# A gated scan feeding a mixture of experts: query transfers issued from GpSimd, a written order of VectorE and ScalarE in the first block, and attention later in ten periods

## The chip, the cores and the metric

The kernel runs on one core of a Trainium2 chip. The metric is the device time of one execution in microseconds (us); smaller is better. The engines of the core are TensorE (PE in the profile, its weight loads PEld), VectorE (DVE), ScalarE (ACT), GpSimd (POOL) and SyncE (SP). SyncE, ScalarE and GpSimd can issue transfers (DMAs); an engine works through its own instructions strictly in the order in which they were queued, and waits where an instruction's inputs are not there.

## What is computed

The reference, cut to what matters. The first part is a linear attention with a complex gate at each step of time, the second a layer of eight experts whose weights are made by eight rounds of normalising rows and columns:

```python
def _attn_ref(q, k, v, a_re, a_im):          # 4 x 8 heads, 768 steps, head dim 48
    mag = np.sqrt(a_re * a_re + a_im * a_im)
    scale = np.minimum(mag, 0.999) / (mag + 1e-06)
    a_re_n, a_im_n = (a_re * scale, a_im * scale)
    for t in range(S):
        ar, ai = (a_re_n[:, :, t, :, None], a_im_n[:, :, t, :, None])
        new_re = ar * S_re - ai * S_im
        new_im = ar * S_im + ai * S_re
        kv = np.einsum('bhd,bhe->bhde', k[:, :, t], v[:, :, t])
        S_re, S_im = (new_re + kv, new_im)
        y[:, :, t] = np.einsum('bhd,bhde->bhe', q[:, :, t], S_re)

def _moe_ref(x, w_gate, w1, w2):             # x: 3072 x 384, 8 experts, 1024 wide
    P = np.exp(x @ w_gate - (x @ w_gate).max())
    for _ in range(8):
        P /= P.sum(1, keepdims=True) + 1e-09
        P /= P.sum(0, keepdims=True) + 1e-09
        P *= N / E
    for e in range(E):
        out += P[:, e:e + 1] * (np.maximum(x @ w1[e], 0.0) @ w2[e])
```

All is in 32-bit floats; a matrix product is made of three products of a high and a low part of its operands.

## The kernel before, in words

**Blocks and periods.** The 3072 tokens are worked through in 12 blocks of 256 (`SUB`), each of two chunks, or halves, of 128 (`CH`). Phase 1 (`phase1`, lines 212 to 305) computes the attention of all blocks and the first two experts; phase 2 (from line 688) does the normalising and the other six experts. Phase 1 goes in periods: period i holds the 16 expert steps of block i-1 (two experts of eight slices) and, between them, the attention of block i.

**What a block's attention needs.** `elem(i)` (line 328) loads gates, queries, keys and values and calls `chain` (line 389), which runs on VectorE and ScalarE: the gates are normalised (lines 402 to 418), multiplied up along time by a scan of complex multiplications (`scan`, `cmul`, lines 307 to 387, temporaries `cm_a` and `cm_b`), and made into scaled keys `kh` (line 436) and queries `z` (line 438). Blocks 0 and 1 do the steps around the scan separately for the two halves, later blocks for both at once.

**The attention itself** is `mix(i)` (line 441), a generator: `next(mix)` emits one piece of it, five for a chunk, ten for a block. For each chunk it moves six pieces of `kh` to `ks` and six of `z` to `qs` by DMA (line 455), all issued by SyncE, keys ahead of queries. `keys(g)` transposes keys for a half g of the heads (line 474) and ScalarE copies them out (`kt`, line 476); `scores(g)` multiplies keys and queries (line 488) and VectorE copies the scores under a mask (line 491, the masked copy); `state(g)` makes the new state's part `U` (line 483); `outs(g)` gives the outputs from masked scores and from the old state (line 505). VectorE then makes the next state (lines 531 to 542), ScalarE writes the outputs' high part `xh` (line 544) and VectorE the low part `xl` (line 545). The pieces are: keys(0) and scores(0); state(0) and keys(1); outs(0) and scores(1); state(1); outs(1) with the state and xh, xl.

**An expert step** is a generator too (`experts`, line 169): nine products of the first layer (`ph`, lines 201 to 203), for each of three column groups one with weights' high part and xh, one with xl, one with the weights' low part and xh; then two activations on ScalarE (`hh`, `hf`) and a subtraction on VectorE (`hl`, line 209). The second layer's six products (`po`, lines 180 to 182) of a step come `LAG` = 3 steps later; three steps are pending at any time. `send((None, 1, None))` emits the second products of one pending step alone.

**The order.** TensorE's instructions keep the program's order (`manual_schedule`, line 114). Those of the other engines are put in order by a planner that simulates the program with its own costs; `issue_after(x)` tells it to put an instruction behind x. `LEAD` (line 27) says at which expert step of period i the pieces of `mix(i)` begin, one behind each step; what is left of the ten when the 16 steps are over comes behind them (line 297), and there, for the blocks named in `LEAD`, second products of a pending step follow each piece while there are any. Before, `LEAD` names blocks 1 to 3 (steps 11, 8 and 5); all others begin at step 4.

**The first block** has no expert steps beside it. Its loop (lines 262 to 280) emits the ten pieces of `mix(0)`, and between them five of the weight splits that `thirds` (line 144) has prepared; three come ahead. A split takes a third of a slice's weights: the load (line 151), a cast to its high part on GpSimd (line 152), two products on TensorE (lines 156 and 157) and a copy of the low part on ScalarE (line 159). `elem(1)` is planned behind block 0's, and `behind` (line 277) puts its twelve complex multiplications behind marks in block 0's masked copies and xl.

Of the kernel before, what the change touches and what calls it, by code (L numbers as in the profile page):

```python
# [60 lines left out]
class Net:  # L61
# [81 lines left out]

    def thirds(self, e, fs, wx, late):
# [3 lines left out]
        def one(t, f, j):  # L148
# [3 lines left out]
            nc.gpsimd.tensor_copy(t[:, 0, cs], raw)  # L152
# [16 lines left out]
    def experts(self):  # L169
# [18 lines left out]
        while True:  # L188
# [10 lines left out]
            for ct in range(NCT):  # L199
                cs = slice(ct * 128, ct * 128 + 128)  # L200
                nc.tensor.matmul(ph, w[:, 0, cs], xh[:, ct, :], start=(ct == 0), stop=False)  # L201
                nc.tensor.matmul(ph, w[:, 0, cs], xl[:, ct, :], start=False, stop=False)  # L202
                nc.tensor.matmul(ph, w[:, 1, cs], xh[:, ct, :], start=False, stop=(ct == NCT - 1))  # L203
# [103 lines left out]
    def cmul(self, L, R, n, alloc):  # L307
# [8 lines left out]
        with ExitStack() as st:  # L316
            if self.behind:
                st.enter_context(self.tc.issue_after(self.behind.pop(0).ins))
            for o, k in ((a, 0), (b, 1)):
                if len(sh) == 4:  # L320
                    V.tensor_tensor(o, L, R[:, k:k + 1].broadcast_to(sh), ALU.mult)
                else:
                    for j in range(2):
                        V.tensor_tensor(o[:, j], L[:, j], R[:, k], ALU.mult)
        V.tensor_tensor(R[:, 0], a[:, 0], b[:, 1], ALU.subtract)
        V.tensor_tensor(R[:, 1], a[:, 1], b[:, 0], ALU.add)
# [62 lines left out]
    def chain(self, i, parts, zt, qk, alloc):  # L389
# [6 lines left out]
        for n in parts or [None]:  # L396
            f0, f1 = (base + i, base + 2 + i) if n else (i, ns + i)
            sq_, x_, y_, zz_, z_ = (t if n is None else half(t, n) for t in (sq, x, y0, zz, z))
            with ExitStack() as st:
# [2 lines left out]
                nc.scalar.activation(sq_, z_, AF.Square, accum_out=fl[:, f0:f0 + 1])
            with ExitStack() as st:
                if i == 2:
                    st.enter_context(tc.issue_after(self.zl[1, 1].ins))
                V.scalar_tensor_tensor(x_, sq_[:, 0], 1e-20, sq_[:, 1], ALU.max, ALU.add)
            with ExitStack() as st:
                if i == 1 and n == 0:
                    st.enter_context(tc.issue_after(self.ev[2].ins))
                nc.scalar.activation(y_, x_, AF.Abs_reciprocal_sqrt)  # L410
            nc.scalar.activation(zz_, y_, AF.Square, accum_out=fl[:, f1:f1 + 1])
            V.tensor_tensor(x_, x_, zz_, ALU.mult)
            V.scalar_tensor_tensor(y_, x_, -3.0, y_, ALU.add, ALU.mult)
# [622 lines left out]
```

## Time and profile before

| | |
|---|---|
| three runs | 1822.3, 1822.61 and 1824.88 us, median 1822.61 |
| the profiled execution | 1822.66 us, its span 1820.8 us |
| mean granted TensorE clock | 0.994 of full speed |
| idle of TensorE by what ended it | queries `qs` 5.4 us in 2 waits, `xl` 5.3 in 4, keys `ks` 4.0 in 1, `xh` 1.9 in 2, masked scores 1.6 in 3 |
| query and key transfers | 144 of each, 64.5 and 64 KB, 2.2 us from issue to landing |
| transfers issued by GpSimd | none |

A line of the timeline gives start and length in us, engine, line of the kernel, operation, output and input, and how many like it were merged (x6); a bracket gives the idle time before it and what ended it. SPq is SyncE's queue of issued transfers: its length is the time that issuing took. A line of the waits gives who waited for whom, in total, how often and the longest. "Granted clock" is the share of TensorE's full speed in a stretch.

### The profile page before, as it was taken

How to read it: one execution, taken by the hardware profiler on the slowest of the kernel's cores; microseconds unless marked ns; L12 is line 12 of the kernel's file. 1: busy time of each engine (PE TensorE's matmuls, PEld its weight loads, DVE VectorE, ACT ScalarE, POOL GpSimd, SP SyncE). 2: the span in 40 equal slices, each digit the busy share in tenths (PEclk: the TensorE clock that was granted, in tenths of full speed). 3: DMA queues.
4: the chain of work that ended last, by engine and by line, in shares of the span. 5: the costliest groups of instructions: out<-in, count | busy, mean ns of one | idle time of the engine just before them, and what ended most of it. 6: DMA issues, size and time to landing. Idle time of an engine off the chain costs nothing.

```text
span 1820.8 us, 30541 instructions
## 1 busy us (share of the span) xinstructions
PE 1765.5 (97%) x12024; PEld 1725.9 (95%) x12024; DVE 1359.6 (75%) x3023; ACT 729.1 (40%) x1592; POOL 16.3 (1%) x29
## 2 busy tenths in 40 slices
PE   5899999999999999999999999999999999999998
PEld 3889899999999999999999999998999999999998
DVE  8899899888873687868575867677776767675754
ACT  7444444554543433334342434243433334242421
POOL 3000000000000000000000000000000000000000
PEclk9999999999999999999999999999999999999999
DMA  6434343333332421401020101231220101020100
GB/s 208 113 108 118 109 115 118 109 107 115 113 102 99 131 87 48 126 18 53 1 70 1 54 17 53 74 105 65 87 70 18 53 18 53 1 70 1 53 27 28
DMA packets 120631, 132.83 MB, mean 73 GB/s; under 512 B 9632, under 2 KB 100512, under 8 KB 120480
## 3 DMA queue, kind: packets, MB, share of 16 engines
q1 hardware_dynamic: 119680, 130.41, 23.4%
q8 instruction: 96, 1.57, 0.4%
q14 instruction: 55, 0.45, 0.1%
q10 hardware_dynamic: 800, 0.39, 0.1%
HBM read 88.22 MB, written 23.59 MB: 61 GB/s over the span
## 4 chain that ended last, share of the span: by engine, by line
PE 83%; DVE 9%; DMA 4%; SPq 1%; issue 1%; ACT 1%; DVEq 0%; ACTq 0%
PE po L761 10%; PE po L759 10%; PE po L760 10%; PE P L798 9%; PE P L800 9%; PE P L799 9%; PE po L180 3%; PE ph L202 3%; PE ph L203 3%; PE ph L201 3%; PE po L182 3%; PE po L181 3%; PE sp L488 2%; PE y L505 2%; DMA raw<-in_w_dram 2%; PE U L483 1%
## 5 line engine op out<-in xcount | busy, mean ns | idle before, releaser
L761 PE MATMUL po<-wc,hl 128*128 128x384 f32 x1152 | 385.3, 334 | 3.0 <-DVE hl L820 3.0
L759 PE MATMUL po<-wc,hh 128*128 128x384 f32 x1152 | 385.0, 334 | 0.1
L760 PE MATMUL po<-wc,hh 128*128 128x384 f32 x1152 | 384.9, 334 | 0.0
L819 ACT ACTIVATE hh<-c 128x384 fp32r<-128x384 f32 x384 | 200.9, 524 | 322.2 <-DVE c L808 320.8
L820 DVE SCALAR_TENSOR_TENSOR hl<-c,hh 128x384 fp32r<-128x384 f32 x384 | 211.9, 552 | 65.9 <-ACT hh L819 58.0
L761 PEld LDWEIGHTS po<-wc,hl 128*128 128x128 f32 x1152 | 216.3, 188 | 4.3 <-DVE hl L820 4.3
L759 PEld LDWEIGHTS po<-wc,hh 128*128 128x128 f32 x1152 | 216.3, 188 | 0.4 <-ACT hh L819 0.4
L760 PEld LDWEIGHTS po<-wc,hh 128*128 128x128 f32 x1152 | 216.3, 188 | 0.0
L813 ACT ACTIVATE s<-P 128x384 f32<-128x384 f32 x192 | 94.2, 490 | 274.2 <-PE P L800 274.2
L207 ACT ACTIVATE hh<-ph 128x256 fp32r<-128x256 f32 x192 | 73.4, 382 | 248.2 <-PE ph L203 247.5
L202 PE MATMUL ph<-xl,w 128*128 128x256 f32 x576 | 163.9, 285 | 5.3 <-DVE xl L545 5.3
L201 PE MATMUL ph<-xh,w 128*128 128x256 f32 x576 | 163.0, 283 | 1.9 <-ACT xh L544 1.9
L203 PE MATMUL ph<-xh,w 128*128 128x256 f32 x576 | 163.2, 283 | 0.0
L798 PE MATMUL P<-B,wa 128*128 128x384 f32 x480 | 160.5, 334 | 1.3 <-DVE u L808 0.7
L800 PE MATMUL P<-B,wa 128*128 128x384 f32 x480 | 160.4, 334 | 0.0
L799 PE MATMUL P<-B,wa 128*128 128x384 f32 x480 | 160.3, 334 | 0.0
L180 PE MATMUL po<-w,hh 128*128 128x384 f32 x384 | 140.7, 366 | 0.9 <-ACT yst L185 0.9
L182 PE MATMUL po<-w,hl 128*128 128x384 f32 x384 | 130.0, 338 | 0.0
L808 DVE TENSOR_TENSOR c<-P,u 128x384 f32<-128x384 f32 x192 | 106.2, 553 | 31.3 <-PE P L800 30.2
L181 PE MATMUL po<-w,hh 128*128 128x384 f32 x384 | 129.4, 337 | 0.0
L808 DVE TENSOR_TENSOR u<-u,s 128x384 f32<-128x384 f32 x96 | 53.3, 556 | 101.0 <-ACT s L813 100.9
L202 PEld LDWEIGHTS ph<-xl,w 128*128 128x128 f32 x576 | 110.0, 191 | 6.2 <-DVE xl L545 6.2
(173 smaller groups left out, 3625.2 us busy)
## 6 DMA issues: line engine op xcount, KB each, us to landing
raw<-in_w_dram SPq DMA_DIRECT2D x48, 768.0 KB, 4.3
qs<-z SPq DMA_DIRECT2D x144, 64.5 KB, 2.2
qk<-in_aqk_dram SPq DMA_DIRECT2D x12, 768.0 KB, 5.0
ks<-kh SPq DMA_DIRECT2D x144, 64.0 KB, 2.2
ye_d<-yst SPq DMA_DIRECT2D x48, 192.0 KB, 1.9
y<-ye_d SPq DMA_DIRECT2D x48, 192.0 KB, 2.4
z<-in_aqk_dram SPq DMA_DIRECT2D x11, 768.0 KB, 7.3
B<-x_d SPq DMA_DIRECT2D x40, 192.0 KB, 3.6
```

The lines of the kernel that those rows point to most:

```text
L180: nc.tensor.matmul(po[k], hh[:, s], w2h, start=f == 0, stop=False)
L201: nc.tensor.matmul(ph, w[:, 0, cs], xh[:, ct, :], start=(ct == 0), stop=False)
L202: nc.tensor.matmul(ph, w[:, 0, cs], xl[:, ct, :], start=False, stop=False)
L203: nc.tensor.matmul(ph, w[:, 1, cs], xh[:, ct, :], start=False, stop=(ct == NCT - 1))
L759: nc.tensor.matmul(po[k], hh[:, s], w2[:, 0, i], start=first, stop=False)
L760: nc.tensor.matmul(po[k], hh[:, s], w2[:, 1, i], start=False, stop=False)
L761: nc.tensor.matmul(po[k], hl[:, s], w2[:, 0, i], start=False, stop=last)
L798: nc.tensor.matmul(ps, t[:, 0, k], x[:, 0], start=first, stop=False)
L799: nc.tensor.matmul(ps, t[:, 0, k], x[:, 1], start=False, stop=False)
L800: nc.tensor.matmul(ps, t[:, 1, k], x[:, 0], start=False, stop=last)
L819: A.activation(hh, c, AF.Relu)
L820: V.scalar_tensor_tensor(hl, c, 0.0, hh.bitcast(F32), ALU.max, ALU.subtract)
```

## The change

Four things are changed.

1. The query transfers are issued from GpSimd's queue, the key transfers stay on SyncE's. Queries of the second chunk are planned behind those of the first. `ql`, behind which later loads are planned, now means the last key transfer.
2. In block 0 (`i == 0`) the pieces are put together anew, four to a chunk: keys(0) and keys(1); scores(0) and state(0); scores(1) and state(1); outs(0) and outs(1) with the rest. The splits come at other places: three ahead, three between the pieces, two behind. The first expert step of each block (`e == 0 and f == 0`) does its six products with xh ahead of the three with xl.
3. Of the twelve casts of the splits the fourth to eighth (`mid`) go from GpSimd to ScalarE. The order of VectorE from block 0's queries to block 1's third complex multiplication, and of ScalarE up to block 0's first `kt`, is written out by hand, with `add_manual_dep` between neighbours; `behind` and the marks go. In this list p0 and p1 are the steps that make keys and queries of block 0's halves, n0 and n1 the normalising of block 1's, m0 and m1 the masked copies, state and xl of block 0's chunks, cm the complex multiplications of block 1.
4. `LEAD` names blocks 1 to 10, with later steps.

```diff
-LEAD = {1: 11, 2: 8, 3: 5}
+LEAD = {1: 13, 2: 13, 3: 12, 4: 11, 5: 9, 6: 8, 7: 7, 8: 6, 9: 6, 10: 5}
...
             nc.sync.dma_start(raw, self.w[e, f, :, cs])
-            nc.gpsimd.tensor_copy(t[:, 0, cs], raw)
+            n = self.nthird
+            self.nthird += 1
+            mid = HEAD <= n < 2 * (LAG + 1)
+            if not mid:
+                nc.gpsimd.tensor_copy(t[:, 0, cs], raw)
 
             def split():
+                if mid:
+                    with self.tc.issue_after(self.kt.ins):
+                        nc.scalar.activation(t[:, 0, cs], raw, AF.Copy)
...
-            for ct in range(NCT):
-                cs = slice(ct * 128, ct * 128 + 128)
-                nc.tensor.matmul(ph, w[:, 0, cs], xh[:, ct, :], start=(ct == 0), stop=False)
-                nc.tensor.matmul(ph, w[:, 0, cs], xl[:, ct, :], start=False, stop=False)
-                nc.tensor.matmul(ph, w[:, 1, cs], xh[:, ct, :], start=False, stop=(ct == NCT - 1))
+            terms = [(ct, k, x) for ct in range(NCT) for k, x in ((0, xh), (0, xl), (1, xh))]
+            if e == 0 and f == 0:
+                terms.sort(key=lambda t: t[2] is xl)
...
-                    if n in (0, 2, 3, 5, 7):
+                    if n in (2, 3, 6):
                         splits.pop(0)()
-                    if n == NF - LAG + 1:
+                    if n == 5:
                         for load in loads:
...
-                with tc.issue_after(self.gl.ins), tc.issue_after(g1.ins):
-                    m = self.marks
-                    self.behind = [m[j] for j in (0, 0, 0, 2, 2, 2, 3, 3, 3, 4, 5, 5)]
+                splits.pop(0)()
+                splits.pop(0)()
+                edge = mybir.DependencyInfo(mybir.DependencyClass.NoSync, mybir.DependencyReason.DATA)
+                with tc.issue_after(g1.ins):
                     self.elem(1)
-                edge = mybir.DependencyInfo(mybir.DependencyClass.NoSync, mybir.DependencyReason.DATA)
+                p0, p1, n0, n1 = (self.dve[k] for k in ((0, 0), (0, 1), (1, "n0"), (1, "n1")))
+                m0, m1, cm = self.dve["m", 0], self.dve["m", 1], self.dve["c"]
+                order = p0 + [n0[0], n1[0]] + p1 + [n0[1], n1[1], n0[2], n1[2], m0[0], n0[3], n1[3], m0[1], n0[4]] + n0[5:]
+                order += m0[2:] + [n1[4], m1[0]] + n1[5:] + cm[:4] + [m1[1]] + cm[4:8] + [m1[-1]] + m1[2:-1] + cm[8:9]
+                for a, b in zip(order, order[1:]):
+                    tc.add_manual_dep(b.ins, a.ins.name, edge, reason="order of VectorE")
+                a0, a1, ev = self.act[1, 0], self.act[1, 1], self.ev[2 * NF + 2:]
+                order = [g1] + ev[:2] + [a0[0], a1[0]] + ev[2:4] + [a0[1], a1[1], a0[2], a1[2]] + ev[4:8] + self.act["kt", 0, 0]
+                for a, b in zip(order, order[1:]):
+                    tc.add_manual_dep(b.ins, a.ins.name, edge, reason="order of ScalarE")
...
+        last = {}
         for c in range(NCH):
...
+            pre = dict(last)
...
-                        dma = nc.sync.dma_start(dst[q:q + D - 2:NCT, :, :w], src[:, a, ct * NCH + c, :w])
-            self.ql[i] = dma
+                        eng = nc.gpsimd if dst is qs else nc.sync
+                        with ExitStack() as st:
+                            if dst is qs and c:
+                                st.enter_context(self.tc.issue_after(pre["q"].ins))
+                            dma = eng.dma_start(dst[q:q + D - 2:NCT, :, :w], src[:, a, ct * NCH + c, :w])
+                        last["q" if dst is qs else "k"] = dma
+                        if dst is ks:
+                            self.ql[i] = dma
...
             keys(0)
+            if i == 0:
+                keys(1)
+                yield
             scores(0)
-            yield
-            state(0)
-            keys(1)
-            yield
-            outs(0)
-            scores(1)
-            yield
+            if i == 0:
+                state(0)
+                yield
+                scores(1)
+            else:
+                yield
+                state(0)
+                keys(1)
+                yield
+                outs(0)
+                scores(1)
+                yield
             state(1)
...
+            if i == 0:
+                outs(0)
             outs(1)
```

The rest of the diff collects the instructions into the lists `dve`, `act` and `ev` from which the two orders are written, and drops the `issue_after` in `cmul` and in the normalising of block 1.

More of the change, by code (lines that the diff above doesn't have):

```diff
@@ L198, in experts @@
             ph = self.psA.tile([128, SUB], F32, tag="ph", name=f"ph{e}_{i}_{f}")
[L199 to L203 removed]
+            terms = [(ct, k, x) for ct in range(NCT) for k, x in ((0, xh), (0, xl), (1, xh))]
+            if e == 0 and f == 0:
+                terms.sort(key=lambda t: t[2] is xl)
+            for q, (ct, k, x) in enumerate(terms):
+                nc.tensor.matmul(ph, w[:, k, ct * 128:ct * 128 + 128], x[:, ct, :], start=q == 0, stop=q == len(terms) - 1)
             hh = self.hp.tile([128, SUB], F32R, tag="hh", name=f"hh{e}_{i}_{f}")
@@ L242, in phase1 @@
         self.xs, self.vt, self.kqd, self.ql, self.sqs, self.zl, self.post = {}, {}, {}, {}, {}, {}, {}
-        self.behind, self.marks, self.ev = [], [], []
+        self.ev, self.dve, self.act, self.nthird = [], {}, {}, 0
         ns = self.N // SUB
@@ L256, in phase1 @@
                 loads.pop(0)()
-        for _ in range(3):
+        for _ in range(HEAD):
             splits.pop(0)()
@@ L315, in cmul @@
         a, b = tmp("a"), tmp("b")
[L316 to L326, printed above, removed]
+        ops = self.dve["c"]
+        for o, k in ((a, 0), (b, 1)):
+            if len(sh) == 4:
+                ops.append(V.tensor_tensor(o, L, R[:, k:k + 1].broadcast_to(sh), ALU.mult))
+            else:
+                for j in range(2):
+                    ops.append(V.tensor_tensor(o[:, j], L[:, j], R[:, k], ALU.mult))
+        ops.append(V.tensor_tensor(R[:, 0], a[:, 0], b[:, 1], ALU.subtract))
+        ops.append(V.tensor_tensor(R[:, 1], a[:, 1], b[:, 0], ALU.add))
     def elem(self, i, scratch=False):
@@ L401, in chain @@
                     st.enter_context(tc.issue_after(self.sqs[1, 1].ins))
[L402 removed]
+                act = self.act[i, n or 0] = [nc.scalar.activation(sq_, z_, AF.Square, accum_out=fl[:, f0:f0 + 1])]
+            ops = self.dve[i, f"n{n or 0}"] = []
             with ExitStack() as st:
@@ L405, in chain @@
                     st.enter_context(tc.issue_after(self.zl[1, 1].ins))
[L406 to L413, printed above, removed]
+                ops.append(V.scalar_tensor_tensor(x_, sq_[:, 0], 1e-20, sq_[:, 1], ALU.max, ALU.add))
+            act.append(nc.scalar.activation(y_, x_, AF.Abs_reciprocal_sqrt))
+            act.append(nc.scalar.activation(zz_, y_, AF.Square, accum_out=fl[:, f1:f1 + 1]))
+            ops.append(V.tensor_tensor(x_, x_, zz_, ALU.mult))
+            ops.append(V.scalar_tensor_tensor(y_, x_, -3.0, y_, ALU.add, ALU.mult))
             self.nrm = nc.scalar.activation(zz_, y_, AF.Square, bias=self.bm05, scale=-0.5e-6)
-            V.tensor_scalar(x_, y_, -0.4995, 1.0, ALU.mult, ALU.min)
-            V.scalar_tensor_tensor(x_, zz_, 0.75, x_, ALU.add, ALU.mult)
+            ops.append(V.tensor_scalar(x_, y_, -0.4995, 1.0, ALU.mult, ALU.min))
+            ops.append(V.scalar_tensor_tensor(x_, zz_, 0.75, x_, ALU.add, ALU.mult))
             for a in range(2):
-                V.tensor_tensor(z_[:, a], z_[:, a], x_, ALU.mult)
+                ops.append(V.tensor_tensor(z_[:, a], z_[:, a], x_, ALU.mult))
+        self.dve["c"] = []
         self.scan(z, alloc)
@@ L483, in state, with scores @@
                     nc.tensor.matmul(U[:, h, :], kts[g][:, j, :], vt[:, c, slot(h):slot(h) + D], start=True, stop=True)
-            def scores(g, i=i, c=c, ks=ks, qs=qs, sss=sss):
+            ops = self.dve["m", i * NCH + c] = []
+            def scores(g, i=i, c=c, ks=ks, qs=qs, sss=sss, ops=ops):
                 sp = self.psS.tile([128, 4, CH], F32, tag="s", name=f"sp{i}_{c}_{g}")
@@ L490, in scores @@
                 self.isc = 1 - self.isc
-                self.marks.append(nc.vector.copy_predicated(ss, self.mask, sp))
+                ops.append(nc.vector.copy_predicated(ss, self.mask, sp))
             def outs(g, c=c, xp=xp, qs=qs, sss=sss, S0=S0, first=first):
@@ L530, in mix @@
                     tm = tmp.tile([SK, H, D], F32, tag="tm", name=f"tm{i}_{c}", bufs=1).rearrange("p (b q) d -> p b q d", b=2)
-                    nc.vector.tensor_tensor(tm, heads(S0), Uv, ALU.add)
+                    ops.append(nc.vector.tensor_tensor(tm, heads(S0), Uv, ALU.add))
                 sa = tmp.tile([SK, H, D], F32, tag="sa", name=f"sa{i}_{c}", bufs=1).rearrange("p (b q) d -> p b q d", b=2)
```

27 lines of the change are left out of this document (15 added, 12 removed).

## The prediction

> **What bounds the kernel now.** The page first: TensorE is busy for nearly all of the span, so time can only be won where it idles or runs slowly.
>
> ```profile
> span 1820.8 us, 30541 instructions
> ...
> PE 1765.5 (97%) x12024; PEld 1725.9 (95%) x12024; DVE 1359.6 (75%) x3023; ACT 729.1 (40%) x1592; POOL 16.3 (1%) x29
> ```
>
> Next the busy time by stretches; the columns are stretch, length, busy time of PE, PEld, DVE, ACT and POOL, granted clock, DMA share and GB/s.
>
> ```profile
> 40.00:68.00 28.00, 17.88 (x193) 15.39 (x194) 26.23 (x69) 9.70 (x27) 1.70 (x4) 0.87 0.56 151
> 68.00:118.00 50.00, 50.00 (x430) 47.93 (x430) 43.82 (x114) 24.75 (x67) 0.00 (x0) 0.97 0.30 86
> 118.00:130.00 12.00, 8.79 (x75) 7.64 (x73) 10.26 (x19) 8.62 (x17) 0.00 (x0) 0.72 0.40 143
> 183.00:191.00 8.00, 5.29 (x30) 5.11 (x29) 6.99 (x20) 1.10 (x3) 0.00 (x0) 0.79 0.40 103
> 220.00:227.00 7.00, 5.20 (x36) 4.94 (x35) 6.94 (x12) 1.76 (x6) 0.00 (x0) 1.00 0.76 243
> 227.00:600.00 373.00, 373.00 (x3489) 360.21 (x3488) 301.40 (x713) 173.33 (x450) 0.00 (x0) 1.00 0.36 108
> ```
>
> From 227 to 600 us TensorE never idles, so there the change can win nothing; it can only lose. The prize lies before: block 0 (40 to 68 us), and four places behind it. Behind block 0 the losses are 12 - 8.79 = 3.2, 8 - 5.29 = 2.7 and 7 - 5.20 = 1.8 us of idling, and what the lower clock takes: 50 x 0.03 = 1.5, 12 x 0.28 = 3.4 and 8 x 0.21 = 1.7 us. VectorE is nearly full in all of them, so the question is whether it can deliver earlier.
>
> The timeline of SyncE (start, length, six transfers merged) and of TensorE (the brackets: idle before, and what ended it) shows block 0:
>
> ```profile
> 37.76 3.94 SPq L455 DMA_DIRECT2D ks<-kh  x6
> 41.80 3.76 SPq L455 DMA_DIRECT2D qs<-z  x6
> ```
> ```profile
> 43.64 0.92 PE L474 MATMUL ktp<-ident,ks 112*128 112x112 f32 x4 [4.04 <-DMA ks<-kh]
> 47.29 2.05 PE L488 MATMUL sp<-qs,ks 112*128 112x128 f32 x8 [2.73 <-DMA qs<-z]
> ...
> 55.87 0.64 PE L505 MATMUL y<-sc,v 128*32 128x128 f32 x16 [0.64 <-DVE sc L491]
> ...
> 63.78 0.43 PE L505 MATMUL y<-sc,v 128*32 128x128 f32 x8 [0.57 <-DVE sc L491]
> ...
> 65.48 0.38 PE L201 MATMUL ph<-xh,w 128*128 128x256 f32 x1 [0.61 <-ACT xh L544]
> 67.67 0.58 PE L202 MATMUL ph<-xl,w 128*128 128x256 f32 x1 [1.81 <-DVE xl L545]
> ```
>
> The scores wait for queries that SyncE issues behind the keys; the outputs wait for masked scores; the experts wait for xh, then for xl. The expert products run steadily from 67.67, with one done before, so I count their start as 67.45.
>
> **Part 1, queries from GpSimd.** SyncE takes 3.76/6 = 0.63 us for each, and the scores start 47.29 - 45.56 = 1.73 us behind the last issue. No transfer of before is issued by GpSimd, so its price, X, is bounded by rows: GpSimd's shortest cast below, and the 2.2 us that a query transfer takes to land, as if each were issued only when the last had landed.
>
> ```profile
> 33.23 5.40 POOL L152 CAST w<-wr 128x256 fp32r<-128x256 f32 x8
> 56.78 0.40 POOL L152 CAST w<-wr 128x256 fp32r<-128x256 f32 x1 [18.16 <-DMA wr<-in_w_dram]
> ```
> ```profile
> qs<-z SPq DMA_DIRECT2D x144, 64.5 KB, 2.2
> ```
>
> So X lies between 0.40 and 2.2 us. I take 0.8: SyncE's 0.63, the only row of the very same transfer, and something for another issuer, an estimate. The Trainium skill (DMA: Bandwidth & Descriptors, "Latency and other measured facts") gives about 1 us to the first byte for transfers that GpSimd issues against 0.6 for SyncE's, because software on GpSimd writes the descriptors; at X = 1.0 the sum below would come out at about 1816.8. No run here shows it yet.
>
> **Part 2, five casts from GpSimd to ScalarE.** The eight casts take 5.40/8 = 0.675 us each where VectorE works beside them, and 0.40 alone. VectorE suffers as much:
>
> ```profile
> 38.28 0.75 DVE L434 SCALAR_TENSOR_TENSOR x<-g,qk 128x384 f32<-128x384 f32 x1
> 38.95 0.54 DVE L438 TENSOR_TENSOR z<-z,qk 128x384 f32<-128x384 f32 x1
> 39.42 0.54 DVE L406 SCALAR_TENSOR_TENSOR x<-sq 128x384 f32<-128x384 f32 x1
> 39.89 0.55 DVE L438 TENSOR_TENSOR z<-z,qk 128x384 f32<-128x384 f32 x1
> ...
> 49.44 0.73 DVE L491 COPY_PREDICATED sc<-mask,sp 128x512 f32<-128x512 uint8 x1 [0.83 <-PE sp L488]
> ```
>
> The step is 38.95 - 38.28 = 0.67 us beside a cast and 39.42 - 38.95 = 0.47 without. With three casts GpSimd is done at 33.23 + 3 x 0.675 = 35.3 instead of 38.63, so some six operations get 0.2 us shorter: VectorE gains 1.2 us. ScalarE has room for the five (9.70 of 28 us busy); were one late, TensorE would wait 0.4 us for it, 2.0 us for all.
>
> **Part 3, block 0.** In the written order VectorE makes half 0's queries without half 1's operations between. The z that ended at 40.44 ends at about 37.5. GpSimd starts at 37.1, needs 6 x 0.8 = 4.8, and 1.73 later, at 43.6, the scores start: 3.7 us earlier. The keys, issued alone by SyncE from 36.3, land by 42. From the scores to the experts it took 67.45 - 47.29 = 20.2 us, with 0.64 + 0.57 + 0.61 + 1.81 = 3.6 idle. With both halves' scores ahead of the outputs, xl right behind xh, and the xh products ahead of the xl ones, I leave 0.5 of it (the last masked copy stands behind the first scan multiply), and take off 0.6 for the transposes now ahead of the scores: 16.5. Start: 43.6 + 16.5 = 60.1, **-7.4 us**. The half-rate stretch behind the old wait goes too: **-1.5**.
>
> What this costs: behind each masked copy in the written order stands all of block 1's chain. VectorE reaches the first at 43.9 and waits to about 45.8, 1.9 instead of 0.83, and about 1.1 more at the later ones; with three more hl of the earlier expert steps (1.0) and less the 1.2 of part 2, block 1's chain comes 2.0 us later.
>
> **Part 4, attention later.** One expert step is 86.67 - 84.50 = 2.17 us, and block 1's attention now stands two steps further back:
>
> ```profile
> 84.50 0.34 PE L180 MATMUL po<-w,hh 128*128 128x384 f32 x1
> ...
> 86.67 0.34 PE L180 MATMUL po<-w,hh 128*128 128x384 f32 x1
> ...
> 95.22 0.55 PE L474 MATMUL ktp<-ident,ks 112*128 112x112 f32 x4
> ```
> ```profile
> 83.39 1.02 DVE L438 TENSOR_TENSOR z<-z,qk 128x384 f32<-128x384 f32 x2
> ```
>
> TensorE gets there at 95.22 + 4.3 - 7.4 - 1.5 = 90.6. Half 0's z ends at 84.41 + 2.0 = 86.4, GpSimd starts on its first part at 85.9, and 4.8 + 1.73 later it is 92.5: a new wait, **+1.9**. Blocks 2 and 3 lie five and seven steps later than before, 10.9 and 15.2 us, so the waits for queries and for VectorE at 183 and 220 go, as does the loss at 118, with its clock: 3.2 + 2.7 + 1.8 + 3.4 + 1.7, **-12.8**.
>
> In return the end of a period is bare. Of ten attention pieces, period 1 now leaves seven for behind the last step, and only three have a second product beside them. What that costs stands at the end of period 1 before, which left five:
>
> ```profile
> 119.29 0.43 PE L505 MATMUL y<-sc,v 128*32 128x128 f32 x8 [0.44 <-DVE sc L491]
> ...
> 121.68 0.38 PE L201 MATMUL ph<-xh,w 128*128 128x256 f32 x1 [1.30 <-ACT xh L544]
> 123.54 0.58 PE L202 MATMUL ph<-xl,w 128*128 128x256 f32 x1 [1.47 <-DVE xl L545]
> ```
>
> The 1.47 is now covered by xh products. The rest, 0.44 + 1.30 = 1.7, is the price of period 4 (five left over). Periods 1 to 3 (seven, seven, six) also lose the second product ahead of the last masked copy, half a step: 2.8 each. Together **+10.1**. A wait of 2.7 us (183) was followed by 1.7 us lost to the clock, one of 1.8 (220) by none, and these are split in two, so I add one such loss: **+1.7**; bounds are none and three. Periods 5 to 7 leave three pieces or fewer, each with a second product: nothing; uncovered they would cost 1.7 each. Blocks 8 to 10 stay within their steps.
>
> **The sum.** -7.4 - 1.5 + 1.9 - 12.8 + 10.1 + 1.7 = -8.0. The profiled execution took 1822.66 us (span 1820.8 and 1.9 around it), the median of the runs is 1822.61: 1814.7 us. Experts and phase 2 behind 600 us shift as they are.
>
> **Rivals.** *GpSimd issues slowly* (slower). At X = 2.2 block 0's second half lands at 37.1 + 12 x 2.2 + 1.73 = 65.2, with 7.2 us of work behind it: experts at 72.4, 12.3 later than forecast; block 1's wait grows by 2.1. Result -8.0 + 14.4 = +6.4: 1829. Between, each 0.1 us costs about 1.0, so it turns at X = 1.6. For it: no row shows this issuer; against: its cast costs it no more than 0.4. Chance 0.12.
>
> *GpSimd's transfers slow VectorE as its casts do.* Twelve transfers of 0.8 us a block beside steps of 0.67: 14 x 0.2 = 2.9 us later for block 1 and again, less slack, for block 2: -8.0 + 2.9 + 2.9, 1820.5. From 227 us VectorE has 72 us to spare, so no more. By the Trainium skill (SBUF — State Buffer, "Who interferes with whom") VectorE operations with two SBUF inputs contend only with GpSimd instructions that read SBUF, and writing descriptors does not; the casts above do read it, and the trace agrees that they collide. By that rule this rival falls. Chance 0.13.
>
> *The bare ends cost double.* The planner may put 0.5 us chain operations ahead of the masked copies, which nothing covers now: three ends of 5.6 with a clock loss each, +8.4 + 3.4, 1826.5 at worst, 1822 at half of it. For it: VectorE is the fullest engine there. Chance 0.18, a third of it slower.
>
> *More is won:* no wait at block 1, ends at 1.7, no clock loss: -8.0 - 1.9 - 3.3 - 1.7, 1807.8. Chance 0.17. The forecast has 0.40.
>
> **How the numbers follow.** A change of 0.2%, 3.6 us, is about what a measurement of this kernel can tell from none. Faster: the forecast, the larger gain and a share of the second rival, 0.61. Slower: the first rival and a third of the third, 0.18. The rest, 0.21, lies within. The range reaches from the larger gain, 1807, to the third rival's worst, 1826; slow issuing is left out.
>
> **What would show it.** Right: GpSimd's issues near 0.8 us, scores at about 43.6 and experts at about 60, block 1's scores waiting some 2 us for queries, idle ends of 2 to 3 us in periods 1 to 3 and none at 183. Wrong: issues above 1.6 us, VectorE steps of 0.67 us beside them, or ends above 5 us.

## The result and the profile after

The changed kernel is slower: median 1834.53 us (1831.88 to 1839.33, six runs) beside 1824.47 for the kernel before (1822.3 to 1825.58, six runs); ratio 1.0061, 95% interval 1.0043 to 1.0079. Forecast were 1814.7 us, range 1807 to 1826. The profiled execution took 1832.53 us, its span 1830.5: 9.7 more than before.

The page of the changed kernel: TensorE does the same work, and GpSimd has the 144 query issues.

```profile
span 1830.5 us, 30689 instructions
...
PE 1767.3 (97%) x12024; PEld 1725.6 (94%) x12024; DVE 1359.2 (74%) x3023; ACT 731.0 (40%) x1597; POOL 89.7 (5%) x168
```

The same stretches as before, columns as before:

```profile
40.00:68.00 28.00, 24.20 (x245) 21.99 (x246) 23.91 (x55) 14.35 (x43) 6.33 (x13) 0.94 0.69 167
68.00:118.00 50.00, 43.12 (x365) 41.32 (x367) 45.22 (x126) 20.91 (x55) 6.25 (x12) 0.90 0.34 78
118.00:130.00 12.00, 9.65 (x105) 8.28 (x93) 10.25 (x20) 8.15 (x19) 0.00 (x0) 0.86 0.36 119
183.00:191.00 8.00, 8.00 (x58) 8.00 (x58) 7.76 (x27) 2.02 (x7) 1.25 (x3) 1.00 0.91 217
220.00:227.00 7.00, 6.31 (x100) 5.45 (x99) 6.95 (x14) 2.32 (x7) 0.40 (x2) 1.00 0.32 99
227.00:600.00 373.00, 364.94 (x3370) 350.78 (x3371) 294.69 (x699) 171.41 (x443) 47.38 (x90) 1.00 0.35 108
```

Block 0 has 6.3 us more of TensorE's work in its 28; the losses at 183 and 220 are gone or smaller. But 68 to 118, where TensorE never idled, now idles 6.9 us at a clock of 0.90 (0.97 before), and 227 to 600, where TensorE never idled, idles 8.1.

Block 0 by SyncE, GpSimd (both chunks) and TensorE:

```profile
36.27 8.35 SPq L476 DMA_DIRECT2D ks<-kh  x12
```
```profile
37.80 3.24 POOL L476 DMA_DIRECT2D qs<-z  x6 [2.60 <-DVE z L453]
42.03 3.12 POOL L476 DMA_DIRECT2D qs<-z  x6 [0.98 <-DVE z L453]
```
```profile
43.60 1.73 PE L497 MATMUL ktp<-ident,ks 112*128 112x112 f32 x8 [1.87 <-DMA ks<-kh]
45.12 1.93 PE L514 MATMUL sp<-qs,ks 112*128 112x128 f32 x8
...
58.61 0.43 PE L531 MATMUL y<-sc,v 128*32 128x128 f32 x8 [1.01 <-DVE sc L517]
...
60.83 0.88 PE L210 MATMUL ph<-xh,w 128*128 128x256 f32 x6
```

X is 3.12/6 = 0.52 us for the second chunk, 3.24/6 = 0.54 for the first. TensorE waits 1.87 us for keys; the scores behind them wait for nothing and start at 45.12. The experts start at 60.83 instead of 67.45, without a wait for xh or xl. Up to here it went nearly as forecast. Then, in period 1 (ScalarE, TensorE, and the window behind):

```profile
77.52 1.58 ACT L439 ACTIVATE sq<-z 128x768 f32<-128x768 f32 x2 [5.31 <-DVE z L341]
...
79.97 0.36 ACT L214 ACTIVATE hh<-ph 128x256 fp32r<-128x256 f32 x1
```
```profile
80.66 0.58 PE L210 MATMUL ph<-xh,w 128*128 128x256 f32 x1 [5.43 <-ACT hf L215]
85.04 0.69 PE L189 MATMUL po<-w,hl 128*128 128x384 f32 x1 [1.45 <-DVE hl L216]
```
```profile
77.70:87.90 10.20, 5.78 (x22) 5.28 (x23) 8.81 (x19) 6.55 (x16) 3.05 (x6) 0.50 0.24 60
```

ScalarE stands still 5.31 us for block 1's scan on VectorE; behind its square is queued the hh of an expert step, and TensorE waits for that. 5.78 us of products then run at half speed, 2.9 us lost.

Later ends and waits of TensorE, in periods 1 to 4, 7 and 9, and a second half-speed stretch:

```profile
120.98 0.42 PE L531 MATMUL y<-sc,v 128*32 128x128 f32 x8 [0.69 <-DVE sc L517]
122.68 0.98 PE L210 MATMUL ph<-xh,w 128*128 128x256 f32 x6 [0.61 <-ACT xh L580]
124.70 0.62 PE L210 MATMUL ph<-xl,w 128*128 128x256 f32 x3 [1.04 <-DVE xl L581]
169.35 0.43 PE L531 MATMUL y<-sc,v 128*32 128x128 f32 x8 [0.78 <-DVE xl L581]
173.49 0.65 PE L531 MATMUL y<-sc,v 128*32 128x128 f32 x8 [1.96 <-DVE sc L517]
176.03 1.65 PE L210 MATMUL ph<-xh,w 128*128 128x256 f32 x6 [0.61 <-ACT xh L580]
226.89 0.96 PE L210 MATMUL ph<-xh,w 128*128 128x256 f32 x6 [0.61 <-ACT xh L580]
229.31 0.62 PE L210 MATMUL ph<-xl,w 128*128 128x256 f32 x3 [1.45 <-DVE xl L581]
252.12 0.44 PE L187 MATMUL po<-w,hh 128*128 128x384 f32 x1 [1.15 <-ACT yst L192]
279.08 0.97 PE L210 MATMUL ph<-xh,w 128*128 128x256 f32 x6 [0.61 <-ACT xh L580]
281.01 0.62 PE L210 MATMUL ph<-xl,w 128*128 128x256 f32 x3 [0.97 <-DVE xl L581]
423.11 0.63 PE L210 MATMUL ph<-xl,w 128*128 128x256 f32 x3 [1.05 <-DVE xl L581]
485.29 0.39 PE L210 MATMUL ph<-xh,w 128*128 128x256 f32 x1 [2.40 <-ACT hf L215]
```
```profile
173.30:180.10 6.80, 5.82 (x48) 4.95 (x49) 6.75 (x11) 2.09 (x4) 2.11 (x5) 0.51 0.58 187
```

The wait at 485.29 is ScalarE's again: there a square stands 3.54 us for its gate load, with hh behind it.

```profile
483.11 1.48 ACT L417 ACTIVATE sq<-z 128x1536 f32<-128x1536 f32 x1 [3.54 <-DMA z<-in_aqk_dram]
...
484.60 0.36 ACT L214 ACTIVATE hh<-ph 128x256 fp32r<-128x256 f32 x1
```

A mark that each period has, the router's first product of a block (lp, second step of the period), shows where time came and went. Before, and after:

```profile
72.42 0.28 PE L556 MATMUL lp<-xh,wgs 128*16 128x256 f32 x1
```
```profile
64.06 0.28 PE L592 MATMUL lp<-xh,wgs 128*16 128x256 f32 x1
```

The first column below is the difference of these two, the next ones how it changes from mark to mark (us, profiled executions). Single executions of one kernel differ by some us (1820.51 to 1828.47 in 29 runs of the kernel before), so the table tells where, and the medians how much.

| kernel | to block 0's mark | period 1 | 2 | 3 | 4 | 5 to 8 | 9 to 11 | sum |
|---|---|---|---|---|---|---|---|---|
| changed | -8.4 | +7.9 | +7.1 | -3.7 | +3.2 | +1.0 | +3.1 | +10.3 |
| e1, ties later | -7.7 | +0.5 | +10.6 | +0.7 | +3.1 | +1.1 | +0.4 | +8.7 |
| e2, queries from SyncE | -3.7 | +9.9 | +7.3 | -3.7 | +3.2 | +1.2 | +5.3 | +19.6 |
| e3, old LEAD | -7.7 | +7.0 | +6.8 | -6.5 | 0.0 | +0.1 | 0.0 | -0.4 |
| e4, new LEAD alone | -0.3 | +0.2 | +9.0 | -0.1 | +4.8 | +12.5 | +2.3 | +28.3 |
| e5, ties later, LEAD 1 to 3 | -9.8 | +0.5 | +10.6 | +0.7 | -0.9 | +0.1 | 0.0 | +1.2 |
| e6, ties later, old LEAD | -5.9 | +9.8 | +5.8 | -6.6 | 0.0 | +0.1 | 0.0 | +3.1 |
| e7, GpSimd queries alone | +1.7 | +1.2 | +7.9 | -6.6 | 0.0 | +0.3 | 0.0 | +4.5 |
| e8, LEAD 4 to 10 | -7.4 | +7.1 | +6.7 | -6.6 | +5.8 | +1.6 | +2.1 | +9.4 |
| g4, LEAD 1 to 3 | -8.5 | +7.9 | +7.1 | -3.7 | -1.0 | +0.3 | 0.0 | +2.2 |
| g1, before, all scans short | -0.4 | +1.3 | -0.9 | -6.4 | +1.7 | +13.3 | +1.8 | +10.4 |
| g2, old LEAD, all scans short | -6.1 | -1.9 | +2.6 | -6.5 | +3.4 | +7.9 | +2.5 | +1.9 |
| g3, changed, all scans short | -4.7 | +4.1 | +2.7 | -3.4 | +2.6 | +1.6 | +1.6 | +4.6 |
| f1, before, scans of 1 to 3 short | -1.3 | +1.3 | -0.6 | -5.7 | 0.0 | 0.0 | 0.0 | -6.3 |
| f2, old LEAD, scans of 1 to 3 short | -8.1 | -1.9 | +2.0 | -6.6 | +0.3 | +0.3 | +1.7 | -12.3 |
| f3, old LEAD, hl on GpSimd | -8.3 | +23.2 | +10.9 | -3.2 | +2.4 | +10.1 | +2.7 | +37.7 |
| f4, before, hl on GpSimd | +0.3 | +3.1 | +5.5 | -3.8 | 0.0 | +0.1 | 0.0 | +5.1 |
| h1, g1 with squares later | -0.7 | +0.2 | -0.3 | -6.6 | 0.0 | +0.4 | +1.2 | -5.8 |
| h2, changed with squares later | -7.6 | +7.9 | +7.3 | -5.3 | +1.9 | +9.5 | +21.9 | +35.6 |

### The profile page after: what moved, and what is told of

Read it like the earlier page. It is cut to its first block, busy times and chain, and to the rows that moved or that the text cites. A ratio compares the mean times of both kernels' runs of the same rounds, so it can differ in the third digit from the quotient of the medians.

```text
span 1830.5 us, 30689 instructions
## 1 busy us (share of the span) xinstructions
PE 1767.3 (97%) x12024; PEld 1725.6 (94%) x12024; DVE 1359.2 (74%) x3023; ACT 731.0 (40%) x1597; POOL 89.7 (5%) x168
## 4 chain that ended last, share of the span: by engine, by line
PE 63%; DVE 6%; DMA 3%; issue 1%; ACT 1%; SPq 0%; DVEq 0%; ACTq 0%
PE po L797 10%; PE po L796 10%; PE po L795 10%; PE P L834 9%; PE P L835 9%; PE P L836 9%; PE ph L210 2%; DMA raw<-in_w_dram 1%; PE po L187 1%; DMA out_dram<-oa 1%; PE po L189 1%; PE po L188 1%; DVE c L844 1%; PE sp L514 1%; DVE tx L672 1%
## 5 line engine op out<-in xcount | busy, mean ns | idle before, releaser
L210 PE MATMUL ph<-xh,w 128*128 128x256 f32 x1152 | 236.0, 285 | 10.3 <-ACT hf L215 7.8
L210 PEld LDWEIGHTS ph<-xh,w 128*128 128x128 f32 x1152 | 191.8, 192 | 12.4 <-ACT hf L215 8.5
```

The source lines that it names most:

```text
L210: nc.tensor.matmul(ph, w[:, k, ct * 128:ct * 128 + 128], x[:, ct, :], start=q == 0, stop=q == len(terms) - 1)
```

## The experiments

**Theories.** T: the loss is period 1's tie. A tie here is an instruction that the program plans behind another. Lines 299 to 309, which the change leaves as they were, plan expert steps 4 and 5 behind the last square and the last z of block 1's two halves, and the squares that come right after its scan behind step 2; expert steps came 7 us earlier, the chain did not. V: VectorE sets the pace up to block 3, so what TensorE gains in block 0 is given back, wherever the wait shows. L: the later attention of blocks 4 to 10 has a price of its own. Rival to all: GpSimd's transfers. The expectations of the first four runs call T theory A; there B is the bare ends of the ten periods, C GpSimd's transfers. For V speaks the stretch from 30 to 180 us, before and after (third number: VectorE): 134.8 and 135.1 of 150 us, for 318 and 317 steps.

```profile
30.00:180.00 150.00, 133.43 (x1178) 123.15 (x1177) 134.84 (x318) 75.97 (x194) 9.71 (x14) 0.94 0.39 114
```
```profile
30.00:180.00 150.00, 129.74 (x1138) 119.35 (x1137) 135.06 (x317) 75.14 (x190) 27.96 (x49) 0.92 0.43 113
```

So do the ends of the chains. The last z of blocks 1, 2 and 3 was ready at 86.6, 135.9 and 179.9 us before, at 87.5, 136.9 and 178.7 after, although the experts had started 6.6 us earlier. Block 3's, before and after:

```profile
178.97 0.95 DVE L438 TENSOR_TENSOR z<-z,qk 128x768 f32<-128x768 f32 x1
```
```profile
177.73 0.95 DVE L453 TENSOR_TENSOR z<-z,qk 128x768 f32<-128x768 f32 x1
```

### One part at a time

**e1**, the ties four steps later (the squares behind step 6, steps 8 and 9 tied):

```diff
-                    if i == 1 and n in (4, 5):
+                    if i == 1 and n in (8, 9):
...
-                if i == 1 and n == 2:
+                if i == 1 and n == 6:
```

> The changed kernel, with two ties of block 1's chain to expert steps moved four steps back: its squares behind step 6 instead of step 2, and steps 8 and 9 instead of 4 and 5 behind its halves. Theory A (ScalarE's queue: the experts start 7 us earlier and the chain ends 5 us later, so steps 4 and 5, which the program still ties behind the chain, wait): the waits of 5.43 and 1.45 us at 75 to 85 us go, and the half-rate stretch behind them, some 10 us: 1823 to 1826. Theory B (the bare ends of ten periods cost it) and theory C (query transfers land later from GpSimd): no more than 3 us, 1829 to 1834.

1831.77 us, ratio 1.0051 (1.0026 to 1.0075). Period 1's wait is gone, period 2 lost 10.6 instead: a wait for queries, then for masked scores behind chain steps.

```profile
149.13 1.13 PE L514 MATMUL sp<-qs,ks 112*128 112x128 f32 x8 [2.27 <-DMA qs<-z]
163.77 0.59 PE L531 MATMUL y<-sc,v 128*32 128x128 f32 x8 [2.62 <-DVE sc L517]
```

The time is that of B and C. The tie is where the loss shows; that T alone does not make it, e5 and g4 below show more cleanly.

**e2**, all transfers from SyncE again: `eng = nc.sync`.

> The changed kernel with the query transfers issued by SyncE again, all else as changed. A: block 0's scores start about 2 us later, step 4 waits all the same, total within 4 us of the changed kernel (1830 to 1836). C: the loss goes, 1822 to 1826. B: no change.

1841.31 us, ratio 1.0098 (1.0074 to 1.0123): slower still, by 4.6 us in block 0 and 2 each in periods 1 and 9. C falls, and the time lies above A's range too. GpSimd's issuing is no cause of the loss: in the changed kernel, where SyncE has the keys in a row, it helps.

**e3**, the changed kernel with `LEAD = {1: 11, 2: 8, 3: 5}`.

> The changed kernel with the old attention steps (blocks 1 to 3 at 11, 8 and 5, all others at 4). A: step 4's wait stays, the 11 us of bare ends in periods 1 to 7 give way to waits for VectorE in blocks 1 to 4: within 5 us of the changed kernel. B: the whole loss goes, 1820 to 1825.

1824.54 us, ratio 0.9997 (0.9984 to 1.0011). As B expected, the whole loss goes: without the later attention the kernel is level with before, and behind 227 us TensorE idles no more:

```profile
227.00:600.00 373.00, 372.98 (x3488) 360.12 (x3487) 299.59 (x711) 173.58 (x450) 44.67 (x84) 1.00 0.36 107
```

Yet block 0's 7.7 us are given back in periods 1 and 2.

**e4**, the kernel before with the new LEAD alone.

> The kernel before with only the later attention steps for ten blocks. By the steps of the prediction (12.8 us of waits gone, 11.8 of bare ends and clock added) within 2 us of before. B: 8 to 11 us slower than before, since the ends are what it pays for. A: within 4 us of before, because the experts of block 0 start late there and no step waits for the chain.

1851.23 us, ratio 1.0159 (1.0129 to 1.0188): none of the three expected so much. Each of periods 1 to 9 ends with a wait for xl, 0.69 to 2.30 us, 14.5 in all; in the changed kernel, with xh products ahead, such waits are 4.5 in all (1.04, 1.45, 0.97 and 1.05). That is a part of the difference; the rest was not taken apart. The longest:

```profile
178.78 0.58 PE L202 MATMUL ph<-xl,w 128*128 128x256 f32 x1 [2.30 <-DVE xl L545]
```

### Which blocks' LEAD, and the ties again

**e5**, e1 with `LEAD = {1: 13, 2: 13, 3: 12}`.

> The changed kernel with two edits: the ties in period 1 stand four steps later (the chain of block 1 behind step 6, steps 8 and 9 behind its squares), and LEAD names only blocks 1 to 3 (13, 13, 12), so that blocks 4 to 10 begin at step 4 as before the change. Theory V (VectorE's chain sets the end of periods 1 to 3, the later attention of blocks 4 to 10 is a loss of its own): the run with the ties alone stood 8.7 us behind at the end of phase 1, of which periods 4, 7 and 9 took 3.1 + 1.4 + 0.4 = 4.9; without them some 4 us slower than before, 1826 to 1829 us. Rival B (the bare ends of periods 1 to 3 are the whole cost, the later blocks only hand it on): no better than with the ties alone, 1831 to 1833. Rival D (blocks 4 to 10 were all): 1822 or less.

1827.47 us, ratio 1.0014 (1.0004 to 1.0024): as V expected. Beside e1, from which it differs by the LEAD of blocks 4 to 10 alone, it is 0.37% faster.

**e6**, e1 with the old LEAD.

> The changed kernel with the ties in period 1 four steps later and LEAD as it was before (11, 8, 5 for blocks 1 to 3). With the old LEAD alone the first block's gain of 7.7 us was given back in period 1 (+7.0) and period 2 (+6.8). Theory V (VectorE has too much to do up to block 3 and gives back what TensorE gains, tied or not): the wait in period 1 goes but period 2 or 3 grows by as much, within -2 to +4 us of before, 1822 to 1828. Theory T (the tie of steps 4 and 5 alone lost it): the gain stays, 6 to 8 us faster, 1816 to 1818.

1826.58 us, ratio 1.0012 (1.0000 to 1.0024). T expected 1816 to 1818 and falls again. The time is V's, the place is not: period 1 itself lost 9.8. Block 1's last z was ready at 91.4 us, 3.2 later than in e3, and TensorE stood 4.22 us ahead of block 1's keys at 95.20.

**e7**, the kernel before with the query transfers from GpSimd and, as in the change, `ql` the last key transfer:

```diff
-                        dma = nc.sync.dma_start(dst[q:q + D - 2:NCT, :, :w], src[:, a, ct * NCH + c, :w])
-            self.ql[i] = dma
+                        dma = (nc.gpsimd if dst is qs else nc.sync).dma_start(dst[q:q + D - 2:NCT, :, :w], src[:, a, ct * NCH + c, :w])
+                        if dst is ks:
+                            self.ql[i] = dma
```

> The kernel before, with the query transfers issued from GpSimd and nothing else changed. Theory of the prediction: the waits for queries in block 0 (2.7 us) and at 183 us (2.7) go and the half-rate stretch behind them (1.7) with them, less what the longer landing (3.8 us instead of 2.2) gives back: 3 to 5 us faster, 1818.5 to 1820.5, scores of the first block at about 45.5 instead of 47.3. Rival: the longer landing eats the head start, queries land as late as before: within 1 us of before. Rival V: queries come sooner but VectorE's masked copies then stand behind its chain: no gain from block 0 and no more than 2 us at 183.

1825.97 us, ratio 0.9997 (0.9988 to 1.0007): no gain, as both rivals expected. From 36 to 50 us the transfers of before landed in 2.2 us, keys and queries alike; issued from two engines at once, they took (size, time to landing):

```profile
qs<-z POOLq DMA_DIRECT2D x12, 64.5 KB, 3.6
ks<-kh SPq DMA_DIRECT2D x12, 64.0 KB, 3.8
```
```profile
45.73 0.98 PE L475 MATMUL ktp<-ident,ks 112*128 112x112 f32 x4 [5.02 <-DMA ks<-kh]
46.50 1.94 PE L489 MATMUL sp<-qs,ks 112*128 112x128 f32 x8
```

TensorE had the keys 2.1 us later than before (43.64), the queries were there; the scores began only 0.8 us sooner (47.29 before), and block 0's mark came 1.7 later. Over the whole execution the median query took 4.4 us to land (3.8 in the changed kernel), the median key 2.3 in both: the queries from GpSimd stay late, the keys on the whole do not. Why was not tried.

**e8**, the changed kernel with 11, 8, 5 for blocks 1 to 3 and the new LEAD for 4 to 10.

> The changed kernel with LEAD as before for blocks 1 to 3 (11, 8, 5) and the later one kept for blocks 4 to 10. By the periods of the changed kernel, periods 4 to 10 took 3.2 + 0.2 - 0.5 + 1.3 + 0.0 + 3.1 = 7.3 us more than before; if these are the later attention's own price, the run stands 7 us behind the changed kernel with the old LEAD throughout (1824.5): 1830 to 1832. Rival: the loss of period 4 and of 9 is handed on from the late blocks 1 to 3, then it stands with the old LEAD's run: 1824 to 1826.

1837.24 us, ratio 1.0068 (1.0051 to 1.0085), above both expectations. The later attention of blocks 4 to 10 costs 12.7 us beside e3, no less than the whole loss of the change.

**g4**, the changed kernel with `LEAD = {1: 13, 2: 13, 3: 12}`.

> The changed kernel with one edit: LEAD names blocks 1 to 3 alone (13, 13, 12), all others begin at step 4 as before; all is computed. If the later attention of blocks 4 to 10 costs what the periods of the changed kernel say (3.2 + 1.3 + 3.1 = 7.6 us) up to what it cost beside the old LEAD (12): 7 to 12 us faster than the changed kernel, 1822 to 1827, and level with before within 3 us. Rival: the ends of periods 1 to 3 are the price (2.8 each by the prediction, and more as measured): 1830 to 1833.

1829.13 us, ratio 1.0021 (1.0009 to 1.0033). From the other side: undoing blocks 4 to 10 wins 1.0061 - 1.0021 = 0.40% (7 us), though the time lies above the 1822 to 1827 expected. L is shown from both sides, 7 to 13 us. The late blocks 1 to 3 cost 1.0021 - 0.9997 = 0.24%, 4 us, beside e3.

Beside e5 only the ties differ, and block 1's squares start at the same time (77.38 in g4, 77.55 in e5). Without the wait period 1 is 7.4 us shorter in e5 and periods 2 and 3 are 7.9 longer; the ratios are 1.0021 and 1.0014. So T alone falls.

### Is it VectorE?

**f1** and **f2**, the kernel before and e3, with `scan` ending after its first three complex multiplications in blocks 1 to 3 (the rest of it is not computed):

```diff
-    def scan(self, z, alloc):
+    def scan(self, z, alloc, short=False):
...
+        if short:
+            return
         ze = zr[:, :, :, TR - 1]
```

> The kernel before with part of the computation left out: in blocks 1, 2 and 3 the scan ends after its first three complex multiplications, which takes 11.2 us of VectorE's steps from each (19.96 to 31.1 us in the first block's scan). Theory V (up to block 3 VectorE's load is what TensorE waits for): the losses behind the first block, 3.2 + 2.7 + 1.8 us idle and 3.4 + 1.7 of clock, go: 9 to 13 us faster, 1812 to 1816. Rival W (they are waits of the written and planned order, at any load): 0 to 4 us faster.

> The changed kernel with the old LEAD and the same part of the scan left out in blocks 1, 2 and 3. With the whole scan the first block's gain of 7.7 us was lost in periods 1 and 2, and the run stood level with before. Theory V: with VectorE relieved the gain is kept, 7 to 8 us faster than the kernel before with the same part left out, 1804 to 1808; the wait of 5.4 us of period 1 (step 4 tied behind block 1's chain) and that of 3.5 at 173 us go. Rival W: the ties and the order lose it at any load, within 3 us of the kernel before with the same part left out.

f1 took 1815.61 us, ratio 0.9953 (0.9936 to 0.9970), f2 1813.77, 0.9947 (0.9931 to 0.9964). f1's time came as V expected, but only in part by its account: the losses at 183 and 220 are gone, that behind 118 is still 2.8 us idle at a clock of 0.86 (3.2 at 0.72 before).

```profile
118.00:130.00 12.00, 9.23 (x83) 8.29 (x82) 11.87 (x22) 4.09 (x12) 0.00 (x0) 0.86 0.69 208
183.00:191.00 8.00, 8.00 (x77) 7.67 (x76) 3.35 (x5) 4.92 (x12) 0.00 (x0) 1.00 0.41 116
```

f2 did not reach its 1804 to 1808. In the profiled executions f2 ends phase 1 6 us ahead of f1, and the tie's wait in period 1 is gone (-1.9 us where e3 had +7.0). But f2's profile is of its fastest execution and f1's of its slowest, and the medians stand only 1.8 us apart, with an interval from some 6 us faster to 3 slower. Not settled by these two.

**g1**, **g2** and **g3**: the kernel before, e3 and the changed kernel, with the scan cut short in blocks 1 to 11.

> The kernel before with part of the computation left out: in blocks 1 to 11 the scan ends after its first three complex multiplications, 11.2 us of VectorE's steps less in each. From 227 us on TensorE never idled before, so little more than with blocks 1 to 3 alone (1815.6): 1813 to 1816. It stands here for what comes next to it.

> The changed kernel with the old LEAD and the same part left out in blocks 1 to 11. Theory V (the first block's gain is given back only because VectorE's chains of the next blocks come no sooner): the gain of 7.7 us is kept, 6 to 8 us faster than the kernel before with the same part left out, 1806 to 1809. Rival W (it is lost to ties, order and the clock at any load): within 3 us of it.

> The changed kernel, with its later attention of blocks 1 to 10, and the same part left out in blocks 1 to 11. Rival L1 (a period that ends with bare attention pieces loses its time by the pieces' own chain of masked copy, output, xh and xl): as with the whole scan, 8 to 12 us slower than with the old LEAD. Rival L2 (it loses only where VectorE's chain steps stand ahead of the masked copies): no more than 3 us slower than with the old LEAD.

1831.84 us, ratio 1.0048 (1.0029 to 1.0067); 1824.76, 1.0003 (0.9990 to 1.0016); 1827.32, 1.0013 (0.9999 to 1.0027). g2 is 7.1 us faster than g1, as V expects and W does not, though neither reached the time expected of it. By the marks, 8.5 us in all, 5.5 are block 0's gain, still there at block 3's mark; the rest comes from periods 4 to 11, where both have losses of another kind (below). So the pair speaks for V, but is not clean. g3 is 2.6 us slower than g2. Its periods 1 to 3 pay 9.2 us more than g2's; periods 4 to 11, where g2 has losses of its own, 8.0 less. That is within L2's 3 us, but with those losses in g2 it does not decide between L1 and L2.

g1 itself was a miss: 11.2 us less work a block for VectorE, and 16 us slower than f1. Its periods 4 to 9 each have a wait of this kind (the first of six, 1.4 to 3.0 us), with the engine behind it:

```profile
233.16 0.39 PE L201 MATMUL ph<-xh,w 128*128 128x256 f32 x1 [1.41 <-ACT hf L208]
```
```profile
230.99 1.49 ACT L404 ACTIVATE sq<-z 128x1536 f32<-128x1536 f32 x1 [5.80 <-DMA z<-in_aqk_dram]
...
232.47 0.36 ACT L207 ACTIVATE hh<-ph 128x256 fp32r<-128x256 f32 x1
```

It is the wait of the changed kernel at 485 us: the next block's square stands on ScalarE ahead of a step's hh while its load is under way.

**h1** and **h2**, g1 and the changed kernel with these squares (blocks 5 and later) planned behind the sixth step:

```diff
+                if n == 5:
+                    self.step5 = self.hf
...
+                if i >= 5:
+                    st.enter_context(tc.issue_after(self.step5.ins))
```

> The kernel before with the scan cut short in blocks 1 to 11 (as in the run that took 1831.8), and with one more edit: the first square of blocks 5 and later is planned behind the activations of the sixth step of the period. Theory S (the square waits for its load at the head of ScalarE's queue, and the expert step's activations behind it): the six waits of 1.4 to 3.0 us on hf at 233, 280, 330, 381, 434 and 482 us go, with the clock behind them, 16.8 us in all by the periods: 1814 to 1818. Rival (the load's lateness costs the time wherever the square stands: the chain comes later and its attention waits): 1828 to 1834.

> The changed kernel with the same edit; all is computed. Theory S: the wait of 2.4 us on hf at 485 us goes, with the 0.7 of clock behind it, and the waits of periods 4 and 7 (xh and xl, bare ends) stay: 2 to 4 us faster than the changed kernel, 1830 to 1832. Rival (the chains of blocks 5 to 11 come later by up to six steps, and their masked copies or queries wait): as slow as the changed kernel or slower, 1834 to 1840.

h1: 1818.19 us, ratio 0.9974 (0.9963 to 0.9985), the six waits gone, 13.7 us faster than g1. Theory S is shown for g1. h2: 1860.47, ratio 1.0201 (1.0184 to 1.0219), 26 us slower than the changed kernel and slower than even its rival expected: the wait at 485 is gone, but with the whole scan the chains come too late, most of all for blocks 9 and 11 (periods 9 and 11 lose 9.0 and 12.7 us), and TensorE waits for keys.

```profile
598.90 0.98 PE L501 MATMUL ktp<-ident,ks 112*128 112x112 f32 x4 [7.41 <-DMA ks<-kh]
```

**f3** and **f4**: e3 and the kernel before with hl of blocks 0 to 2 on GpSimd.

```diff
-            nc.vector.tensor_tensor(hl, hf, hh.bitcast(F32), ALU.subtract)
+            (nc.gpsimd if i in (0, 1, 2) else nc.vector).tensor_tensor(hl, hf, hh.bitcast(F32), ALU.subtract)
```

> The changed kernel with the old LEAD, and the subtraction hl of the expert steps of blocks 0 to 2 (periods 1 to 3) made by GpSimd in VectorE's place; all is computed. It takes 16 steps of some 0.5 us, 8 us a period, from VectorE. Theory V: VectorE's chains come earlier and the first block's gain is kept: 5 to 8 us faster than before, 1817 to 1820. Rival S (GpSimd's two reads slow VectorE's steps from 0.47 to 0.67 us as its casts did): what is saved is given back, within 3 us of before, or slower.

> The kernel before with the same subtractions of periods 1 to 3 made by GpSimd; all is computed. Theory V: part of the losses at 118, 183 and 220 us (7.7 idle, 5.1 of clock) goes, 3 to 8 us faster, 1817 to 1822. Rival S: VectorE's steps beside them are longer, within 3 us of before, or slower.

1856.44 us, ratio 1.0175 (1.0158 to 1.0193), and 1829.52, 1.0037 (1.0021 to 1.0053): both slower. VectorE and GpSimd of f4, side by side:

```profile
98.28 0.55 DVE L321 TENSOR_TENSOR cm_b<-z 128x384 f32<-128x384 f32 x1
...
100.49 1.10 DVE L321 TENSOR_TENSOR cm_b<-z 128x384 f32<-128x384 f32 x1
```
```profile
100.41 0.76 POOL L209 TENSOR_TENSOR hl<-hf,hh 128x256 fp32r<-128x256 f32 x1 [2.47 <-ACT hf L208]
```

A VectorE step of 0.55 us takes 1.10 beside GpSimd's subtraction. VectorE is spared 0.42 us (its own mean for hl) and loses 0.55 here: from 30 to 180 us it is busy 138.3 us for 286 steps in f4, 134.8 for 318 before. Nothing is relieved, and the results come later (mean 1.0 us instead of 0.42). Rival S of these two runs came out (it is another than theory S of h1). By the Trainium skill (SBUF — State Buffer, "Who interferes with whom") VectorE operations with two SBUF inputs contend with GpSimd instructions that read SBUF; here the trace agrees, 1.10 us beside 0.55. In f3 the queries are on GpSimd's queue as well, and hl stands behind them; how much of its 32 us that is was not tried; 23 of them stand in period 1.

## Why the prediction was wrong

**Right.** Block 0: forecast -7.4 and -1.5 for the clock behind it, together -8.9 at the mark, measured -8.4; experts forecast 60.1, measured 60.83; half 0's z forecast 37.5, measured 37.6. GpSimd's transfers do not slow VectorE: two steps beside them took 1.02 us, 0.47 a step.

```profile
42.12 1.02 DVE L425 TENSOR_TENSOR x<-x,zz 128x384 f32<-128x384 f32 x2
```

The xh products cover xl in block 0. The bare ends of periods 1 to 3 idled 0.69 + 0.61 + 1.04 = 2.3, 0.78 + 1.96 + 0.61 = 3.4 and 0.61 + 1.45 = 2.1, forecast 2.8 each; period 4's 0.61 + 0.97 = 1.6, forecast 1.7.

**Mis-sized, without weight.** X: 0.52 to 0.54 us, taken 0.8. What came in its place was not priced: landings of 3.4 us in block 0 instead of 2.2, so that the keys, "landed by 42", kept TensorE waiting 1.87 to 43.6, and the scores began at 45.12 instead of 43.6. That the experts still came near their time is partly luck: from scores to experts it took 15.7 us, forecast 16.5. In the third rival "1822 at half of it" is a slip: half of 8.4 + 3.4 gives 1820.6.

**Failed: "a new wait, +1.9".** Period 1 had no wait for queries; block 1's z of half 0 was ready at 84.65, not 86.4. It had 5.43 + 1.45 of idling behind the unchanged tie and 2.9 of clock: 9.8. The sum moved expert steps 7.4 us forward and never asked which of them are tied, by their number, to a chain that stays where it is.

**Failed: "-12.8".** The waits at 118, 183 and 220 were read as lateness that an attention further back leaves behind. 183 and 220 did go (period 3: -3.7), but more came at 80 and 173: VectorE's chains of blocks 1 to 3 ended when they had ended before, so TensorE, 7 us earlier, waited for them elsewhere; e1, e3, e5, e6 and e7 only chose the place. With less for VectorE to do the losses at 183 and 220 go as well (f1). Most of the one at 118 stays even then; what makes it is open. The clock was sized too low besides: one loss of 1.7 was forecast, and 1.7 came at 124 and 3.3 behind 173 (6.8 us at 0.51). Over periods 1 to 3 the forecast was +1.9 - 12.8 + 8.4 + 1.7 = -0.8, measured +11.3.

**Failed: "Periods 5 to 7 ... nothing", "Blocks 8 to 10 stay within their steps".** Periods 4 to 11 cost 7.3 us in the profile (forecast 1.7, for period 4), 7 to 13 in g4 and e8: uncovered ends in 4 and 7, a step's products waiting 1.15 for ScalarE in 4, and in 9 the square that waits for a load. The price of 1.7 for an uncovered end stood in the prediction, and was set to nothing for period 7.

**The rivals.** Slow issuing and slowed VectorE fell. "Bare ends cost double" named VectorE's chain ahead of masked copies, which is what 173.49 shows, but put a bound of 1826.5 on it and left the tie and the later blocks out.

**Open.** Why periods 4 and later cost 7 us by one pair of runs and 13 by the other; how much of block 0's gain VectorE's relief would save (f1 and f2 leave it open by their medians, and e3 with the edits of h1 was not run); and why block 8's later attention should be what delays the load at 478, which fits the buffers but was not tried by itself. No run beat the kernel before with the whole computation.

## What to carry to other kernels

Before you count an earlier start as won, add up the fullest other engine over the whole stretch: here, where it was busy 135 of 150 us on both sides, the gain came back as a wait elsewhere, and moving the wait did not remove it. When a change shifts one engine, list every tie by step number that the diff leaves alone, and each instruction that waits at the head of an in-order queue with another's work behind it (a square that waits for a load, with the activations TensorE needs next). Price late work at the end of each period, with what covers it, even where nothing idled before: there it can only lose.

## What was unexpected in the hardware

GpSimd issued a transfer in 0.52 to 0.54 us, SyncE in 0.63 to 0.70, but issued from both at once in block 0 the same 64 KB transfers landed in 3.4 to 3.8 us instead of 2.2. A wait of 2.0 us (173.49) was followed by 5.8 us of products at half speed, as was one of 5.4; ends with waits of 0.6 to 1.5 us were followed by none at 229 and 281, but by 1.7 us lost at 124, where the waits were no longer. And a subtraction moved to GpSimd took from VectorE what it had saved.
